# A turn of q moved ahead of the last half of w3, and the softmax sums of chunk 1 spread over the first down steps

## The chip, the cores and the metric

The kernel runs on one core of one Trainium2 chip. The core has a matrix engine (TensorE, PE in the profile), a vector engine (VectorE, DVE), a scalar engine for functions such as exp and ln (ScalarE, ACT), a general engine that here only issues loads and stores (GpSimd, POOL), a sync engine that issues transfers (SyncE, SP), and 16 DMA engines that move data between the chip's main memory and the on-chip memory. Matmuls write into PSUM, an accumulator memory of 8 banks, each 512 fp32 columns wide on 128 partitions; ScalarE and VectorE carry results from there to the on-chip memory. The metric is the time of one execution in microseconds, as the device measures it: a median of several runs, lower is better.

## The reference

Two stages follow each other: attention with projected keys and values, then a feed-forward layer that takes the maximum of three products.

```python
# q, k, v: (8 batches, 8 heads, 1024, 64) fp32;  E, F: (64, 1024)
k_proj = einsum('ks,bhsd->bhkd', E, k)             # 1024 keys become 64
v_proj = einsum('ks,bhsd->bhkd', F, v)
scores = matmul(q, k_proj.transpose(0, 1, 3, 2)) / 8
attn   = exp(scores - max);  attn = attn / (sum(attn) + 1e-9)
x      = matmul(attn, v_proj)                      # -> (8192 tokens, 512)
h      = maximum(maximum(x @ w1, x @ w2), x @ w3)  # w1, w2, w3: (512, 768)
out    = h @ w_out                                 # w_out: (768, 512)
```

## The kernel before: the parts that matter here

Each batch of 1024 tokens is worked off in two chunks of 512. From chunk 1 of batch 0 on there is a steady order: 18 steps of four matmuls (`l1`), four `down` steps, and between them, at fixed slots, the attention of the next batch. Chunk 0 of batch 0 has a path of its own, so that the matrix engine can start while the inputs still arrive. All loads that convert fp32 to bf16 go through one queue, in the order in which GpSimd issues them:

```python
for wt, w in zip(w_sb[1:], (w2, w3)):              # w2, w3 in halves of 256 rows
    for hh in range(2):
        nc.gpsimd.dma_start(out=wt[:, 2 * hh:2 * hh + 2, :], in_=w[hh * 256:(hh + 1) * 256]...)
# ... cut
nc.gpsimd.dma_start(out=q_1, in_=qv_[1])           # q of batch 0, chunk 1
for x in range(2):
    nc.gpsimd.dma_start(out=wo_sb[:, 3 * x:3 * x + 3], in_=...)   # w_out in halves
load(1, k, k_t); load(1, v, v_t); load(1, q, q_t)  # batch 1
```

The attention of chunk 1 of batch 0 has four parts. q is turned (d onto the partitions) by matmuls with the identity, into banks 4 to 7, and copied out:

```python
def q_up0():
    for g in range(NPAIR):                         # 4 pairs of heads: 32 matmuls in all
        for sl in range(4):
            for u in range(2):
                nc.tensor.matmul(out=ps[u * D:(u + 1) * D, 4 + g, sl * P:(sl + 1) * P],
                                 lhsT=q_1[:, HEAD[2 * g + u], sl, :], rhs=ident, ...)
    for j in range(2):                             # line 279: two banks in each copy
        nc.scalar.copy(out=qT[0][:, 4 + 2 * j:6 + 2 * j]..., in_=ps[:, 4 + 2 * j:6 + 2 * j, :]...)

def scores_up0():
    for g, bank in ((0, 4), (1, 5), (2, 6), (3, 7)):
        scores0(1, g, bank)                        # line 249, two matmuls each
    for g in (0, 2):                               # line 286, exp
        nc.scalar.activation(out=pT[:, g:g + 2, 1, :], in_=ps[:, 4 + g:6 + g, :], func=AF.Exp, scale=scale)

def sums0(ch, bank):
    quads0(ch, bank, lambda rows, g: ones[rows, :])                        # line 229
    nc.scalar.activation(out=lns[ch], in_=ps[:, bank:bank + 2, :], func=AF.Ln)          # line 257
    nc.scalar.activation(out=rinv[ch], in_=lns[ch], func=AF.Exp, scale=-1.0)            # line 258

def av_up0():
    for f, bank in enumerate((6, 4)):
        quads0(1, bank, lambda rows, g: vp2[0][rows, g, f, :])             # line 229
    norm0(1, 0, 6, (0, 1))                         # line 268, VectorE: xT = ps * rinv
    norm0(1, 1, 4, (0, 1))
```

The w2 and w3 steps of chunk 0 work in halves of the contraction, because the weights arrive in halves: first all steps with half 0, then with half 1, and a step that is complete goes to VectorE (line 405) and then ticks a slot.

```python
def l1_first(i, jts, banks):
    for hh in range(2):
        for jt, bank in zip(jts, banks):
            for ct in (2 * hh, 2 * hh + 1):
                nc.tensor.matmul(out=ps[:, bank, :], lhsT=w_sb[i][:, ct, ...], rhs=xT[0][:, ct, 0, :], ...)   # line 402
            if hh:
                nc.vector.tensor_tensor(out=h1c[jt] if i == 1 else hT[0][:, jt, :], ..., op=ALU.max)
                yield
```

Then comes `down` of chunk 0 in two halves of its contraction (`down_half`, line 216): four tiles of tokens with the first three tiles of h, then the same four with the last three. The slots at which the parts of attention go between:

```python
groups = [(10, q_up0), (11, scores_up0), (13, lambda: sums0(1, 4)), (15, av_up0),
          (19, g1[0]), (22, lambda: q_pe1(0)), (24, lambda: q_pe1(1)), (25, g1[1]), ...]   # g1: batch 1
...
for i, jts, banks in ((1, range(6), (6, 7, 0, 1, 4, 5)), (2, range(3), (2, 3, 6)), (2, range(3, 6), (0, 1, 2))):
    for _ in l1_first(i, jts, banks):
        tick()
state["f"] = 2
for x in range(2):
    for tt in range(4):
        down_half(tt, x)                           # bank (3 + tt) % 4
        if x:
            tick()
```

`g1[0]` is `kv` of batch 1 (lines 116 and 118): 16 matmuls into bank 4, which ScalarE and VectorE then empty in four copies (lines 122, 123, 125, 126). `q_pe1` turns half of the heads of batch 1's q with 16 transposes into banks 4 and 5 (line 299).

Of the kernel before, what the change touches and what calls it, by code (L numbers as in the profile page):

```python
# [16 lines left out]
def kernel(ctx: ExitStack, tc: tile.TileContext, q, k, v, E, F, w1, w2, w3, w_out, out):  # L17
    nc = tc.nc
# [13 lines left out]
    def T(shape, dt, name):  # L32
        return sb.tile(shape, dt, name=name)

    ps = pp.tile([P, 8, 512], FP32, name="ps")
# [7 lines left out]
    w_sb = [T([P, NCT, DF], BF16, f"w{i}_sb") for i in range(3)]  # L43
# [6 lines left out]
    qT = [T([P, H, SI // 2, P], BF16, f"qT{i}") for i in range(NB)]  # L50
# [20 lines left out]
    q_1 = q_t[0].rearrange("p h si d -> p (h si d)")[:, 4 * H * D:].rearrange("p (h n d) -> p h n d", h=H, d=D)  # L71
# [17 lines left out]
    def load_behind_turn(b, order="qkv"):  # L89

        nc.gpsimd.tensor_copy(out=seen, in_=kpT[(b - 1) % NB][:, 0, 0:1])
        for c in order:
            load(b, *{"q": (q, q_t), "k": (k, k_t), "v": (v, v_t)}[c])

    def q_turn(b, hs):
        nc.sync.dma_start_transpose(
            out=qT[b % NB][:, hs].rearrange("p h s t -> p (h s) t"),
            in_=q_t[b % NB][:, hs].rearrange("p h si d -> p (h si d)"),
        )
# [70 lines left out]
    state = {"f": 0, "n": 0}  # L170
# [40 lines left out]

    def down_half(tt, x):

        bank = (3 + tt) % 4
        for jt in range(3 * x, 3 * x + 3):
            nc.tensor.matmul(out=ps[:, bank, :], lhsT=hT[0][:, jt, tt * P:(tt + 1) * P],  # L216
                             rhs=wo_sb[:, jt, :], start=(jt == 0), stop=(jt == NJT - 1))
        if x:
            nc.scalar.copy(out=o_acc[0][:, tt, :], in_=ps[:, bank, :])
            if tt % 2 == 1:  # L220
                nc.gpsimd.dma_start(out=out_0[0][:, tt - 1:tt + 1, :], in_=o_acc[0][:, tt - 1:tt + 1, :])


    def quads0(ch, bank, lhs, hhs=(0, 1)):
        for hh, j, g, u in QUADS:
            if hh not in hhs:
                continue
            rows = slice(u * KP, (u + 1) * KP)
            nc.tensor.matmul(out=ps[j * HD:(j + 1) * HD, bank + hh, :], lhsT=lhs(rows, g),
                             rhs=pT[rows, g, ch, :], start=True, stop=True, tile_position=(u * KP, j * HD))  # L230
# [24 lines left out]
    def sums0(ch, bank):  # L255
        quads0(ch, bank, lambda rows, g: ones[rows, :])
        nc.scalar.activation(out=lns[ch], in_=ps[:, bank:bank + 2, :], func=AF.Ln)
        nc.scalar.activation(out=rinv[ch], in_=lns[ch], func=AF.Exp, scale=-1.0)  # L258
# [7 lines left out]
    def norm0(ch, half, bank, hhs):  # L266
        for hh in hhs:
            nc.vector.tensor_tensor(out=xT[0][:, 2 * hh + half, ch, :], in0=ps[:, bank + hh, :],  # L268
                                    in1=rinv[ch][:, hh * 512:(hh + 1) * 512], op=ALU.mult)


    def q_up0():
        for g in range(NPAIR):
            for sl in range(4):
                for u in range(2):
                    nc.tensor.matmul(out=ps[u * D:(u + 1) * D, 4 + g, sl * P:(sl + 1) * P], lhsT=q_1[:, HEAD[2 * g + u], sl, :],
                                     rhs=ident, start=True, stop=True)
        for j in range(2):
            nc.scalar.copy(out=qT[0][:, 4 + 2 * j:6 + 2 * j].rearrange("p h s t -> p (h s t)"),
                           in_=ps[:, 4 + 2 * j:6 + 2 * j, :].rearrange("p b n -> p (b n)"))  # L280

    def scores_up0():
        for g, bank in ((0, 4), (1, 5), (2, 6), (3, 7)):
# [4 lines left out]
    def av_up0():  # L288
        for f, bank in enumerate((6, 4)):
            quads0(1, bank, lambda rows, g: vp2[0][rows, g, f, :])  # L290
        norm0(1, 0, 6, (0, 1))
        norm0(1, 1, 4, (0, 1))


    def q_pe1(hh):
        for h in range(4 * hh, 4 * hh + 4):
            for sp in range(SI // 2):
                o = (h % 2) * 512 + sp * P
                nc.tensor.transpose(out=psb[:, AB + (h % 4) // 2, o:o + P],  # L299
                                    in_=q_t[1][:, h, 2 * sp:2 * sp + 2, :].rearrange("p s d -> p (s d)"), identity=ident)  # L300
        for j in range(2):
            (nc.vector.tensor_copy if j else nc.scalar.copy)(
                out=qT[1][:, 4 * hh + 2 * j:4 * hh + 2 * j + 2].rearrange("p h s t -> p (h s t)"), in_=psb[:, AB + j, :])
# [10 lines left out]
    qv_ = q[0].rearrange("h (ch p n) d -> ch p h n d", ch=2, p=P)  # L314
# [17 lines left out]
            load0(v, v_t, NPAIR - 1)  # L332
    for wt, w in zip(w_sb[1:], (w2, w3)):
        for hh in range(2):
            nc.gpsimd.dma_start(out=wt[:, 2 * hh:2 * hh + 2, :],
                                in_=w[hh * 256:(hh + 1) * 256].rearrange("(r f) n -> r f n", f=2))
    nc.vector.memset(ones, 1.0)  # L337
# [57 lines left out]
            nc.tensor.matmul(out=ps[:, W1B[jt], :], lhsT=w_sb[0][:, ct, jt * P:(jt + 1) * P], rhs=xT[0][:, ct, 0, :],  # L395
                             start=(ct == 0), stop=(ct == NCT - 1))

    def l1_first(i, jts, banks):
        for hh in range(2):
            for jt, bank in zip(jts, banks):  # L400
                for ct in (2 * hh, 2 * hh + 1):
                    nc.tensor.matmul(out=ps[:, bank, :], lhsT=w_sb[i][:, ct, jt * P:(jt + 1) * P], rhs=xT[0][:, ct, 0, :],  # L402
                                     start=(ct == 0), stop=(ct == NCT - 1))
                if hh:
                    nc.vector.tensor_tensor(out=h1c[jt] if i == 1 else hT[0][:, jt, :], in0=ps[:, bank, :], in1=h1c[jt],
                                            op=ALU.max)
                    yield
# [1 line left out]
    def av0(f, hh):  # L409
        quads0(0, 6 + f - hh, lambda rows, g: vp2[0][rows, g, f, :], (hh,))  # L410

    nc.gpsimd.dma_start(out=q_1, in_=qv_[1])
    for x in range(2):
        nc.gpsimd.dma_start(out=wo_sb[:, 3 * x:3 * x + 3], in_=w_out.rearrange("(jt p) m -> p jt m", p=P)[:, 3 * x:3 * x + 3])
    load(1, k, k_t)
# [28 lines left out]
    for b in range(B):  # L444
        groups = attention(b + 1, turn_dma) if b + 1 < B else []
        if b == 0:
            g1 = [g for _, g in groups]
            groups = [(10, q_up0), (11, scores_up0), (13, lambda: sums0(1, 4)), (15, av_up0),
                      (19, g1[0]), (22, lambda: q_pe1(0)), (24, lambda: q_pe1(1)), (25, g1[1]), (28, g1[2]),
                      (31, g1[3]), (32, g1[4]), (33, g1[5]), (34, g1[6]), (36, g1[7])]  # L450
        slot = 0
        gi = 0

        def tick():
            nonlocal slot, gi
            slot += 1
            while gi < len(groups) and groups[gi][0] <= slot:
                groups[gi][1]()
                gi += 1
            if b == 0:  # L460
                if slot == 22:
                    load_behind_turn(2, "kvq")
                if slot == 28:
                    q_turn(2, slice(0, H // 2))
                return
            if b == 1 and slot == 3:
                q_turn(2, slice(H // 2, H))
            if b + 2 < B:
                if slot == 9:
                    load_behind_turn(b + 2)  # L470
                if slot == 18:
                    q_turn(b + 2, slice(0, H // 2))
                if slot == 27:
                    q_turn(b + 2, slice(H // 2, H))

        for ch in range(2):
            c = 2 * b + ch
            if c == 0:
                for i, jts, banks in ((1, range(6), (6, 7, 0, 1, 4, 5)), (2, range(3), (2, 3, 6)), (2, range(3, 6), (0, 1, 2))):
                    for _ in l1_first(i, jts, banks):  # L480
                        tick()
                state["f"] = 2
                for x in range(2):
                    for tt in range(4):
                        down_half(tt, x)
                        if x:
                            tick()
                continue
            for s in range(18):
                l1(b, ch, c, s // 3, s % 3)  # L490
                tick()
                if pend and s in (2, 5, 8, 11):
                    pend.pop(0)()
                    tick()
            pend = [lambda tt=tt, b=b, ch=ch, c=c: down(b, ch, c, tt) for tt in range(4)]
        if b == 0:
            while pend:
                pend.pop(0)()
                tick()
# [32 lines left out]
```

The softmax here doesn't subtract the row's maximum and nothing guards it: scores larger than these inputs give would overflow.

## Time and profile before

| what | value |
|---|---|
| time, median of 3 runs | 401.62 us (401.57 to 401.82) |
| span of the profiled execution | 399.6 us |
| matrix engine busy | 392.9 us, 98% of the span |
| VectorE, ScalarE busy | 185.8 us, 166.5 us |
| granted clock of the matrix engine | 1.00 |
| the longest waits of matmuls | for VectorE's `ones` 1.2 us (1 time), for line 268 1.2 us (2 times) |

In a timeline, a row holds the start and the duration of a run of equal instructions in microseconds, the engine, the line of the kernel, the operation, the tiles that it writes and reads, and how many there are. In brackets stands how long the engine had been idle before, and what ended that. Matmuls are pipelined, so the durations of neighbouring rows overlap; the distance between two starts tells what a run costs. In the list of transfers, the last number is the time from issue to landing.

### The profile page before, as it was taken

The numbers are of one execution on the slowest core, as the hardware profiler recorded it, in microseconds if no ns is written. First come the engines' busy times: TensorE is split into PE (matmuls) and PEld (weight loads), VectorE is DVE, ScalarE is ACT, GpSimd is POOL, SyncE is SP. The second block draws the span as 40 slices with busy tenths as digits, with TensorE's granted clock in tenths as the row PEclk, the third lists the DMA queues.
The fourth block names the chain that finished last, engine by engine and source line by source line (L and its number), as shares of the span: only waits on it lengthen the run. The fifth ranks groups of instructions, "written<-read, shape, count | busy, mean of one in ns | idle before, by whom it ended". The sixth has DMA issues, their size and how long they took to land.

```text
span 399.6 us, 6013 instructions
## 1 busy us (share of the span) xinstructions
PE 392.9 (98%) x2432; PEld 170.0 (43%) x2432; DVE 185.8 (46%) x268; ACT 166.5 (42%) x250; POOL 71.6 (18%) x110
## 2 busy tenths in 40 slices
PE   8999899999999999999999999999999999999996
PEld 4444353444444444444444444444444444444443
DVE  3346355553744265433844256443655337433441
ACT  4413457347325552247223652245532472222222
POOL 7352140150002401060000600024010000000000
PEclk9999999999999999999999999999999999999999
DMA  8999969999922997259930899129991111102022
GB/s 219 206 209 205 206 170 204 228 146 179 181 91 66 168 179 181 64 97 192 226 121 13 166 196 219 53 65 175 216 137 62 59 52 54 52 2 105 1 107 105
DMA packets 62667, 53.73 MB, mean 134 GB/s; under 512 B 30512, under 2 KB 57648, under 8 KB 62640
## 3 DMA queue, kind: packets, MB, share of 16 engines
q0 software_dynamic: 31776, 43.52, 54.1%
q1 hardware_dynamic: 30032, 8.92, 15.8%
q10 hardware_dynamic: 832, 0.92, 0.7%
q8 instruction: 19, 0.31, 0.3%
q14 instruction: 8, 0.07, 0.0%
HBM read 57.15 MB, written 16.78 MB: 185 GB/s over the span
## 4 chain that ended last, share of the span: by engine, by line
PE 92%; DMA 4%; DVE 1%; ACT 1%; issue 1%; POOL 0%; POOLq 0%; DVEq 0%
PE ps L179 59%; PE ps L203 19%; PE ps L116 3%; PE ps L145 3%; PE ps L402 3%; DMA w_sb<-in_moe_w_dram 2%; DMA k_t<-in_k_dram 2%; PE ps L135 2%; PE ps L395 1%; PE ps L216 1%; DVE xT L160 1%; DVE xT L268 0%; PE ps L299 0%; PE ps L196 0%; ACT rinv L258 0%
## 5 line engine op out<-in xcount | busy, mean ns | idle before, releaser
L179 PE MATMUL ps<-xT,w_sb 128*128 128x512 bf16 x1080 | 246.6, 379 | 1.2 <-DVE xT L268 1.2
L179 PEld LDWEIGHTS <-w_sb 128*128 128x128 bf16 x1080 | 103.1, 98 | 133.9 <-issue 14.0
L184 DVE TENSOR_TENSOR m<-ps,h1s 128x512 f32<-128x512 f32 x90 | 62.2, 691 | 143.0 <-PE ps L179 114.8
L203 PE MATMUL ps<-wo_sb,hT 128*128 128x512 bf16 x354 | 85.5, 379 | 0.0
L182 ACT COPY h1s<-ps 128x512 f32<-128x512 f32 x90 | 52.8, 587 | 66.1 <-PE ps L179 65.8
L205 ACT COPY o_acc<-ps 128x512 f32<-128x512 f32 x59 | 34.6, 587 | 97.8 <-PE ps L203 97.8
L210 POOL DMA_DIRECT2D out_dram<-o_acc x28 | 20.1, 718 | 272.3 <-ACT o_acc L205 269.2
L186 DVE TENSOR_TENSOR hT<-ps,m 128x512 bf16<-128x512 f32 x90 | 62.3, 692 | 13.7 <-PE ps L179 5.2
L203 PEld LDWEIGHTS <-hT 128*128 128x128 bf16 x354 | 33.6, 98 | 44.1 <-issue 5.4
L160 DVE TENSOR_TENSOR xT<-ps,rinv 128x1024 bf16<-128x1024 f32 x28 | 32.9, 1217 | 7.8 <-PE ps L145 7.8
L138 ACT ACTIVATE pT<-ps 128x1024 bf16<-128x1024 f32 x28 | 27.1, 1021 | 13.3 <-PE ps L135 13.3
L87 POOL DMA_DIRECT2D v_t<-in_v_dram x21 | 15.3, 755 | 3.3 <-PE ps L402 2.5
L152 ACT ACTIVATE lns<-ps 128x1024 f32<-128x1024 f32 x14 | 13.6, 1021 | 1.9 <-PE ps L145 1.9
L155 ACT ACTIVATE rinv<-lns 128x1024 f32<-128x1024 f32 x14 | 14.2, 1061 | 0.0
L116 PE MATMUL ps<-k_t,eT 128*64 128x512 bf16 x56 | 13.4, 382 | 0.0
L118 PE MATMUL ps<-v_t,fT 128*64 128x512 bf16 x56 | 13.4, 382 | 0.0
L87 POOL DMA_DIRECT2D q_t<-in_q_dram x14 | 10.7, 770 | 3.9 <-DMA q_t<-in_q_dram 1.7
L87 POOL DMA_DIRECT2D k_t<-in_k_dram x14 | 10.6, 766 | 2.2 <-ACT o_acc L441 1.2
L402 PE MATMUL ps<-xT,w_sb 128*128 128x512 bf16 x48 | 10.9, 379 | 0.0
L122 ACT CAST kp<-ps 64x512 bf16<-64x512 f32 x7 | 4.1, 580 | 15.9 <-PE ps L118 15.9
L307 PE MATMUL ps<-warm 128*128 128x512 bf16 x26 | 9.4, 469 | 1.2 <-DVE ones L337 1.2
L123 DVE CAST kp<-ps 64x512 bf16<-64x512 f32 x7 | 4.8, 682 | 12.1 <-ACT kp L122 12.1
(84 smaller groups left out, 155.4 us busy)
## 6 DMA issues: line engine op xcount, KB each, us to landing
out_dram<-o_acc POOLq DMA_DIRECT2D x30, 512.0 KB, 3.3
q_t<-in_q_dram POOLq DMA_DIRECT2D x15, 512.0 KB, 8.8
k_t<-in_k_dram POOLq DMA_DIRECT2D x14, 512.0 KB, 13.3
v_t<-in_v_dram POOLq DMA_DIRECT2D x18, 256.0 KB, 17.5
v_t<-in_v_dram POOLq DMA_DIRECT2D x7, 512.0 KB, 16.8
w_sb<-in_moe_w_dram POOLq DMA_DIRECT2D x4, 384.0 KB, 10.2
k_t<-in_k_dram POOLq DMA_DIRECT2D x4, 256.0 KB, 8.1
w_sb<-in_moe_w_dram POOLq DMA_DIRECT2D x4, 192.0 KB, 9.8
```

Of the source, the lines that this page charges most:

```text
L87: nc.gpsimd.dma_start(out=dst[b % NB][:, slots], in_=sv[:, heads])
L116: nc.tensor.matmul(out=ps[0:KP, AB, :], lhsT=eT[:, si, :], rhs=k_t[i][:, :, si, :], start=(si == 0), stop=(si == SI - 1))
L138: nc.scalar.activation(out=pT[:, 2 * u + gg, :, :], in_=ps[:, AB + 2 * gg:AB + 2 * gg + 2, :], func=AF.Exp, scale=scale)
L160: nc.vector.tensor_tensor(out=xT[b % 3][:, 2 * u + half, :, :], in0=ps[:, AB + 2 * u:AB + 2 * u + 2, :], in1=rinv[u].rearrange("p (c n) -> ...
L179: nc.tensor.matmul(out=ps[:, bank, :], lhsT=w_sb[i][:, ct, jt * P:(jt + 1) * P], rhs=xT[b % 3][:, ct, ch, :], start=(ct == 0), stop=(ct == ...
L182: nc.scalar.copy(out=h1s[jt % 2], in_=ps[:, bank, :])
L184: nc.vector.tensor_tensor(out=m12[jt % 2], in0=ps[:, bank, :], in1=h1s[jt % 2], op=ALU.max)
L186: nc.vector.tensor_tensor(out=hT[c % 2][:, jt, :], in0=ps[:, bank, :], in1=m12[jt % 2], op=ALU.max)
L203: nc.tensor.matmul(out=ps[:, bank, :], lhsT=hT[c % 2][:, jt, tt * P:(tt + 1) * P], rhs=wo_sb[:, jt, :], start=(jt == 0), stop=(jt == NJT - 1))
L205: nc.scalar.copy(out=o[:, tt, :], in_=ps[:, bank, :])
L210: nc.gpsimd.dma_start(out=dst[:, tt - 1:tt + 1, :], in_=o[:, tt - 1:tt + 1, :])
L402: nc.tensor.matmul(out=ps[:, bank, :], lhsT=w_sb[i][:, ct, jt * P:(jt + 1) * P], rhs=xT[0][:, ct, 0, :], start=(ct == 0), stop=(ct == NCT ...
```

## The change

The change moves work in the first 50 us, with the same instructions in all but one place. The half of q for chunk 1 is loaded ahead of the last half of w3, so that it can be turned within the first w3 steps, after their first half of the contraction. The second of the two copies of turned q goes to VectorE. Scores follow the first three w3 steps, sums come after the last w3 step, and AV stands between the two halves of down. The aim is that exp, ln and normalisation of chunk 1 lie beside w3 and down matmuls. Banks are dealt anew so that banks 4 to 7 stay free for the attention meanwhile, and `kv` of batch 1 goes one slot later.

```diff
 def down_half(tt, x):
-        bank = (3 + tt) % 4
+        bank = tt
 ...  (q_up0)
         for j in range(2):
-            nc.scalar.copy(out=qT[0][:, 4 + 2 * j:6 + 2 * j]..., in_=ps[:, 4 + 2 * j:6 + 2 * j, :]...)
+            (nc.vector.tensor_copy if j else nc.scalar.copy)(
+                out=qT[0][:, 4 + 2 * j:6 + 2 * j]..., in_=ps[:, 4 + 2 * j:6 + 2 * j, :]...)
 ...  (loads)
     for wt, w in zip(w_sb[1:], (w2, w3)):
         for hh in range(2):
+            if wt is w_sb[2] and hh:
+                nc.gpsimd.dma_start(out=q_1, in_=qv_[1])
             nc.gpsimd.dma_start(out=wt[:, 2 * hh:2 * hh + 2, :], ...)
 ...
-    def l1_first(i, jts, banks):
+    def l1_first(i, jts, banks, between=None):
         for hh in range(2):
+            if hh and between:
+                between()
 ...
-    nc.gpsimd.dma_start(out=q_1, in_=qv_[1])
 ...  (slots)
-            groups = [(10, q_up0), (11, scores_up0), (13, lambda: sums0(1, 4)), (15, av_up0),
-                      (19, g1[0]), (22, lambda: q_pe1(0)), (24, lambda: q_pe1(1)), (25, g1[1]), ...
+            groups = [(9, scores_up0), (12, lambda: sums0(1, 4)), (20, g1[0]), (22, lambda: q_pe1(0)),
+                      (24, lambda: q_pe1(1)), (25, g1[1]), ...
 ...
-                for i, jts, banks in ((1, range(6), (6, 7, 0, 1, 4, 5)), (2, range(3), (2, 3, 6)), (2, range(3, 6), (0, 1, 2))):
-                    for _ in l1_first(i, jts, banks):
+                for part in ((1, range(6), (6, 7, 0, 1, 4, 5)), (2, range(3), (2, 3, 0), q_up0), (2, range(3, 6), (1, 2, 3))):
+                    for _ in l1_first(*part):
                         tick()
-                state["f"] = 2
+                state["f"] = 3
                 for x in range(2):
+                    if x:
+                        av_up0()
                     for tt in range(4):
                         down_half(tt, x)
```

More of the change, by code (lines that the diff above doesn't have):

```diff
@@ L278, in q_up0 @@
         for j in range(2):
-            nc.scalar.copy(out=qT[0][:, 4 + 2 * j:6 + 2 * j].rearrange("p h s t -> p (h s t)"),
-                           in_=ps[:, 4 + 2 * j:6 + 2 * j, :].rearrange("p b n -> p (b n)"))
+            (nc.vector.tensor_copy if j else nc.scalar.copy)(
+                out=qT[0][:, 4 + 2 * j:6 + 2 * j].rearrange("p h s t -> p (h s t)"),
+                in_=ps[:, 4 + 2 * j:6 + 2 * j, :].rearrange("p b n -> p (b n)"))
     def scores_up0():
@@ L447 @@
             g1 = [g for _, g in groups]
-            groups = [(10, q_up0), (11, scores_up0), (13, lambda: sums0(1, 4)), (15, av_up0),
-                      (19, g1[0]), (22, lambda: q_pe1(0)), (24, lambda: q_pe1(1)), (25, g1[1]), (28, g1[2]),
+            groups = [(9, scores_up0), (12, lambda: sums0(1, 4)), (20, g1[0]), (22, lambda: q_pe1(0)), (24, lambda: q_pe1(1)), (25, g1[1]), (28, g1[2]),
                       (31, g1[3]), (32, g1[4]), (33, g1[5]), (34, g1[6]), (36, g1[7])]
```

## The prediction

> **What bounds the kernel now.** I read the page first: the busy shares and the chain that ended last.
>
> ```profile
> PE 392.9 (98%) x2432; PEld 170.0 (43%) x2432; DVE 185.8 (46%) x268; ACT 166.5 (42%) x250; POOL 71.6 (18%) x110
> PE 92%; DMA 4%; DVE 1%; ACT 1%; issue 1%; POOL 0%; POOLq 0%; DVEq 0%
> ```
>
> TensorE is busy 98% of the span and carries 92% of the chain. So a change pays only through the time in which TensorE stands still, and all of that is near the start (a table by stretches gives 42.05 us busy of 42.10 from 57.9 to 100 us, then 100.00 of 100.00 twice). I therefore read TensorE's timeline of the stage that the diff touches: w2 and w3 steps, turn of q, scores, down, sums, AV, then chunk 1.
>
> ```profile
> 25.09 9.66 PE L402 MATMUL ps<-xT,w_sb 128*128 128x512 bf16 x44
> 34.69 1.08 PE L276 MATMUL ps<-ident,q_t 128*64 128x128 bf16 x32
> 35.70 0.60 PE L402 MATMUL ps<-xT,w_sb 128*128 128x512 bf16 x2
> 36.43 0.62 PE L249 MATMUL ps<-qT,kpT 64*64 64x512 bf16 x4
> 37.34 0.62 PE L249 MATMUL ps<-qT,kpT 64*64 64x512 bf16 x4 [0.29 <-ACT qT L279]
> 37.89 0.61 PE L402 MATMUL ps<-xT,w_sb 128*128 128x512 bf16 x2
> 38.34 3.40 PE L216 MATMUL ps<-wo_sb,hT 128*128 128x512 bf16 x15
> 41.67 0.41 PE L229 MATMUL ps<-pT,ones 64*32 64x512 bf16 x8
> 42.01 1.47 PE L216 MATMUL ps<-wo_sb,hT 128*128 128x512 bf16 x6
> 43.41 0.62 PE L229 MATMUL ps<-pT,vp 64*32 64x512 bf16 x16
> 43.97 0.82 PE L216 MATMUL ps<-wo_sb,hT 128*128 128x512 bf16 x3
> 45.15 0.38 PE L179 MATMUL ps<-xT,w_sb 128*128 128x512 bf16 x1 [0.36 <-DVE xT L268]
> 46.35 2.70 PE L179 MATMUL ps<-xT,w_sb 128*128 128x512 bf16 x11 [0.82 <-DVE xT L268]
> ```
>
> The durations overlap, so I count from start to start. The chain view gives 44 w2/w3 matmuls in 9.50 us, 0.216 us each. Dense cost from 25.26 us (where the chain puts the first w2 matmul) to the kv projection of batch 1 (49.05 us): 48 of w2/w3 10.36, turn 35.70-34.69 = 1.01, scores 2 x 0.55 (37.34 to 37.89) = 1.10, sums 0.34, AV 0.56, 24 down 5.18, 12 of chunk 1 2.59; together 21.14 us. The stretch takes 23.79, so 2.65 us are bubbles: 0.30 and 0.36 around the scores, 0.53 and 0.98 before the first two chunk 1 matmuls, and the rest small change at switches of operation. The two large ones end in the normalisation (DVE, line 268). Its own wait is in the next two views (ScalarE, then VectorE):
>
> ```profile
> 35.36 1.93 ACT L279 CAST qT<-ps 128x1024 bf16<-128x1024 f32 x2 [9.58 <-PE ps L276]
> 42.26 1.03 ACT L257 ACTIVATE lns<-ps 128x1024 f32<-128x1024 f32 x1
> 43.32 1.06 ACT L258 ACTIVATE rinv<-lns 128x1024 f32<-128x1024 f32 x1
> ...
> 44.41 2.48 DVE L268 TENSOR_TENSOR xT<-ps,rinv 128x512 bf16<-128x512 f32 x4 [5.18 <-ACT rinv L258]
> ```
>
> The sums ended at 42.01, so Ln, Exp and normalisation need until 46.89, while TensorE had only 9 down matmuls and AV to lay beside them.
>
> The change also swaps two loads, so I read issue-to-landing of single loads, in a short window each. The last half of w3 (384 KB, issued at 18.46 us), then the half of q (512 KB, 19.80 us):
>
> ```profile
> w_sb<-in_moe_w_dram POOLq DMA_DIRECT2D x1, 384.0 KB, 11.3
> ...
> q_t<-in_q_dram POOLq DMA_DIRECT2D x1, 512.0 KB, 12.7
> ```
>
> They landed at 29.76 and 32.50. The same reading gives 27.9 for w3's first half, 34.3 and 36.3 for w_out's halves, 46.5 for the last part of batch 1's v, 49.1 and 51.6 for its q: one unbroken stream, 1.9 us for 384 KB and 2.6 to 2.7 for 512 KB.
>
> **What the Trainium skill says.** "DMA: Bandwidth & Descriptors", section "Two DMAs through the same engine are not ordered": within one queue of one engine, descriptors start in order. The landings above are in the order of issue, so I let the two loads change places in the stream. "TensorE: Matmul & The Clock Gate", section "Back-to-back issue gap": about 216 ns for 512 columns on the warm clock; the trace has 0.216 us. "TensorEngine Tiling (Array Packing)", section "PSUM Bottleneck": use both ScalarE and VectorE to empty PSUM; that is what the split copy of turned q does, and before, ScalarE alone took 1.93 us for the pair. "PSUM — Partial Sum Buffer", section "Terms": two engines may not touch the same bank and quadrant at once. The trace agrees in so far as the readers of the kv bank go strictly one after another (below).
>
> **The change part by part.**
>
> Loads. The half of q goes in front of the last half of w3. It should land at 27.9 + 2.65 = 30.5 us, w3's half where q was, 32.4 to 32.5; w_out and all of batch 1 keep their times.
>
> Turn. It moves from behind 44 to behind 30 w2/w3 matmuls: 25.26 + 30 x 0.216 = 31.74 us. q is there since 30.5. Its second bank holds the last w2 step, which VectorE frees at 32.07 (its two L405 steps start at 30.79 and take 1.28), while TensorE wants it at 32.0: about 0.1 us lost. The turn ends near 32.85. The first w3 matmul of the second half needs w3 at 32.5: slack of 0.35 us.
>
> Copies. ScalarE takes 0.97 us (half of 1.93), about 32.6 to 33.6. VectorE's 128x1024 copy of fp32 has no row yet; a 1024-wide normalisation from PSUM takes 1217 ns on L160, and at 512 columns its copy (0.68) and its product (0.69) cost the same, so I estimate 1.2 us: 33.05 to 34.25. The six w3 matmuls between end at 34.15, and the third head pair, first to need the second copy, comes at 34.7. So the bubbles at the scores (0.66 us) go. The w3 maxima wait behind VectorE's copy, to about 36.2; the bank of the first is wanted again near 35.7 and is free by 35.0.
>
> Sums and AV. Scores end near 35.3, the last 12 w3 matmuls near 37.9, sums at 38.2. Both exponentials are done at about 36.9, so sums don't wait. Then 12 down matmuls (2.59 us) to 40.8; the Ln and Exp (2.1 us, from 38.35) end at 40.45 beside them. AV to 41.4, VectorE normalises from 41.2 to 43.7, and the second 12 down matmuls run to 44.0. So chunk 1's first matmul finds its columns: the two bubbles before it (1.51 us) go.
>
> Sum. The dense cost to kv with the 16 chunk 1 matmuls that now stand ahead of it is 22.0 us (21.14 + 4 x 0.216): 25.26 + 22.0 = 47.26, and I add 0.35 for the bank and the switches of operation: 47.6. Before, the same work would have been done at 49.05 + 0.86 = 49.9. Gain 2.3 us at this point.
>
> **What is given back.** After kv its bank is emptied by four copies in turn:
>
> ```profile
> 50.94 0.58 ACT L122 CAST kp<-ps 64x512 bf16<-64x512 f32 x1 [2.99 <-PE ps L118]
> 52.27 0.37 ACT L125 CAST vp<-ps 64x256 bf16<-64x256 f32 x1 [0.75 <-DVE kp L123]
> ...
> 51.55 0.68 DVE L123 CAST kp<-ps 64x512 bf16<-64x512 f32 x1 [1.76 <-ACT kp L122]
> 52.66 0.42 DVE L126 CAST vp<-ps 64x256 bf16<-64x256 f32 x1 [0.43 <-ACT vp L125]
> ```
>
> The bank is free at 53.08, 2.25 us behind kv's end (50.83). Then the turn of batch 1's q by TensorE writes it, and before, 12 matmuls (2.59 us) stood between. Now kv comes four matmuls later and the turn does not, so 8 are left, 1.73 us: TensorE waits about 0.5 us there. Net gain 2.3 - 0.5 = 1.8 us. Behind it the order is the same, TensorE has no bubble to lose, and loads and stores hang on the same slots: batch 2's last part of v landed at about 69 us for a kv at 76.3. So 1.8 us should reach the end: 401.6 - 1.8 = 399.8 us.
>
> **The rivals.**
> 1. The w3 load takes the place of the wait removed. For it: only 0.35 us of slack, and if w3 landed at 33.5 everything behind would move 0.65 us. Against: its place in the stream is fixed by bytes already measured. It would make 400.1 to 400.8.
> 2. Batch 1's loads become the bound. For it: kv moves from 49.05 to 47.6, and v lands at 46.5, a slack of 1.1 us; q lands at 49.1 for a turn at about 51.7. Against: both still fit. If the stream slipped by 2 us, kv would wait 0.9: 400.7.
> 3. The kv bank costs nothing, because VectorE's and ScalarE's copies come sooner than I think: gain 2.3, 399.3.
> 4. A copy on VectorE that takes much longer than 1.2 us delays scores and w3 maxima together: each 0.5 us over costs up to 0.5; I see nothing for it.
>
> **Range and chances.** The bubbles that the change can reach add up to 2.65 us, so 399.0 is a floor. Rivals 1 and 2 together cost about 1.5, which would leave a small gain; a loss needs more than one of them to be worse than worked out. I take 399.8 with 399.1 to 400.8. 2% is 8 us and no part of this stage holds so much: within 2% 0.985, faster 0.01, slower 0.005.
>
> **What would show it.** Right: no wait of chunk 1's first matmuls for line 268; the turn at 31.7 to 32 us, straight behind w2 and the first w3 half; Ln and Exp beside the first 12 down matmuls; kv's first matmul at about 47.6; a wait of 0.4 to 0.6 us before the first transpose of batch 1's q; the same distance from there to the end as before. Wrong: a TensorE wait for w_sb or q_t near 32.5 us, kv waiting for v_t, scores waiting for the VectorE copy by more than 0.3 us, or a new bubble behind 60 us.

## The result: 399.98 us, and the profile after

| | before | changed |
|---|---|---|
| time, median of 6 runs | 401.66 us (401.56 to 402.22) | 399.98 us (399.53 to 400.54) |
| changed / before | | 0.9958 (95% interval 0.9945 to 0.9971) |
| span of the profiled execution | 399.6 us | 398.1 us |

The changed kernel is 1.7 us, 0.4%, faster. Measured again beside other kernels it gave 0.9963 (0.9950 to 0.9976).

The page of the changed kernel, busy shares:

```profile
PE 392.5 (99%) x2432; PEld 170.0 (43%) x2432; DVE 186.9 (47%) x269; ACT 166.0 (42%) x249; POOL 71.6 (18%) x110
```

TensorE does the same work (392.5 us against 392.9) in a shorter span. Where the time came from is read in its timeline of the changed stage; lines 407, 276, 249, 229, 216 and 179 are w2 and w3 steps, turn, scores, sums or AV, down, and chunk 1; 116 and 300 are kv and the turn of batch 1's q. (An edit that adds or takes lines shifts these numbers by a few, so w3 steps are line 402 before and 405 or 408 in some experiments.)

```profile
25.15 6.64 PE L407 MATMUL ps<-xT,w_sb 128*128 128x512 bf16 x30
31.72 1.32 PE L276 MATMUL ps<-ident,q_t 128*64 128x128 bf16 x32
32.97 1.47 PE L407 MATMUL ps<-xT,w_sb 128*128 128x512 bf16 x6
34.37 1.05 PE L249 MATMUL ps<-qT,kpT 64*64 64x512 bf16 x8
35.35 2.76 PE L407 MATMUL ps<-xT,w_sb 128*128 128x512 bf16 x12
38.05 0.41 PE L229 MATMUL ps<-pT,ones 64*32 64x512 bf16 x8
38.39 2.76 PE L216 MATMUL ps<-wo_sb,hT 128*128 128x512 bf16 x12
41.08 0.62 PE L229 MATMUL ps<-pT,vp 64*32 64x512 bf16 x16
41.64 2.76 PE L216 MATMUL ps<-wo_sb,hT 128*128 128x512 bf16 x12
44.24 3.62 PE L179 MATMUL ps<-xT,w_sb 128*128 128x512 bf16 x16
47.79 0.40 PE L116 MATMUL ps<-k_t,eT 128*64 128x512 bf16 x1
...
49.64 1.90 PE L179 MATMUL ps<-xT,w_sb 128*128 128x512 bf16 x8
51.95 1.05 PE L300 MATMUL ps<-ident,q_t 128*128 128x128 bf16 x16 [0.42 <-DVE vp L126]
```

No row from 25 us on has a bracket until the last one: the two waits for the normalisation (0.36 and 0.82 us before) and the wait for the copy (0.29) are gone, and a new one stands before the turn of batch 1's q. ScalarE's and then VectorE's timeline show why the first chunk 1 matmul finds its columns:

```profile
38.53 1.02 ACT L257 ACTIVATE lns<-ps 128x1024 f32<-128x1024 f32 x1 [1.56 <-PE ps L229]
39.58 1.06 ACT L258 ACTIVATE rinv<-lns 128x1024 f32<-128x1024 f32 x1
...
33.07 1.22 DVE L279 CAST qT<-ps 128x1024 bf16<-128x1024 f32 x1 [0.95 <-PE ps L276]
41.62 2.49 DVE L268 TENSOR_TENSOR xT<-ps,rinv 128x512 bf16<-128x512 f32 x4 [2.45 <-PE ps L229]
```

Ln and Exp end at 40.6 us, beside the first 12 down matmuls, and VectorE waits for AV (2.45 us idle), no longer for Exp. It ends at 44.11, before chunk 1 begins at 44.24. The transfers, half of q issued at 18.52 us and last half of w3 at 19.85, each in a window of its own:

```profile
q_t<-in_q_dram POOLq DMA_DIRECT2D x1, 512.0 KB, 12.1
...
w_sb<-in_moe_w_dram POOLq DMA_DIRECT2D x1, 384.0 KB, 12.6
```

They land at 30.6 and 32.45 us: q 1.1 us ahead of its turn, w3 0.5 us ahead of its use (32.97).

The profiles begin this stage at slightly different times (25.09 us before, 25.15 after, 24.76 to 25.74 in the experiments other than w3_late); the last section comes back to this. So I compare the stretch from the first w2 matmul to the second turn of batch 1's q, behind which all orders are the same: 25.09 to 56.05 before, 30.96 us; 25.15 to 54.57 after, 29.42 us. From there to the end of the span it is about 343.5 us in both (the span is given to 0.1 us). The whole gain of the profiled execution is in that stretch: 1.54 us.

### The profile page after: what moved, and what is told of

It is laid out like the page before. It is cut to its first block, busy times and chain, and to the rows that moved or that the text cites. A ratio compares the mean times of both kernels' runs of the same rounds, so it can differ in the third digit from the quotient of the medians.

```text
span 398.1 us, 6013 instructions
## 1 busy us (share of the span) xinstructions
PE 392.5 (99%) x2432; PEld 170.0 (43%) x2432; DVE 186.9 (47%) x269; ACT 166.0 (42%) x249; POOL 71.6 (18%) x110
## 4 chain that ended last, share of the span: by engine, by line
PE 95%; DMA 2%; DVE 1%; ACT 0%; POOL 0%; issue 0%; POOLq 0%; DVEq 0%
PE ps L179 59%; PE ps L203 19%; PE ps L116 3%; PE ps L145 3%; PE ps L407 2%; DMA k_t<-in_k_dram 2%; PE ps L135 2%; PE ps L398 1%; PE ps L216 1%; PE ps L308 1%; PE ps L229 1%; DVE xT L160 1%; PE ps L249 1%; PE ps L300 0%; PE ps L242 0%; PE ps L196 0%
## 5 line engine op out<-in xcount | busy, mean ns | idle before, releaser
L152 ACT ACTIVATE lns<-ps 128x1024 f32<-128x1024 f32 x14 | 13.6, 1022 | 1.9 <-PE ps L145 1.9
```

## The experiments

All start from the changed kernel. "Stretch" is the one just described, from one profile of each kernel; the changed kernel has 29.42 us in both of its profiles. Ratios are to the kernel before on the same chip.

| run | time, us | ratio to before (95%) | stretch, us | against changed |
|---|---|---|---|---|
| sums_late | 401.83 | 1.0002 (0.9994 to 1.0011) | 31.09 | +1.67 |
| turn_late | 401.08 | 0.9990 (0.9981 to 0.9999) | 30.51 | +1.09 |
| loads_back | 400.54 | 0.9973 (0.9962 to 0.9983) | 30.01 | +0.59 |
| kv19 | 399.36 | 0.9945 (0.9930 to 0.9960) | 28.84 | -0.58 |
| copy_act | 400.11 | 0.9957 (0.9940 to 0.9973) | 29.42 | 0.00 |
| w3_late | 427.13 | 1.0627 (1.0606 to 1.0647) | not comparable | |
| turn_order | 399.47 | 0.9941 (0.9926 to 0.9957) | 29.18 | -0.24 |
| kv19_order | 399.46 | 0.9940 (0.9922 to 0.9959) | 28.80 | -0.62 |
| w3_behind_wo | 401.49 | 0.9996 (0.9986 to 1.0005) | 30.89 | +1.47 |
| kv18 | 400.05 | 0.9959 (0.9944 to 0.9974) | 29.93 | +0.51 |
| four_first | 399.56 | 0.9947 (0.9929 to 0.9964) | 28.61 | -0.81 |
| after_again | 400.39 | 0.9963 (0.9950 to 0.9976) | 29.42 | 0.00 |

**sums_late: sums and AV back to their old slots**

```diff
-groups = [(9, scores_up0), (12, lambda: sums0(1, 4)), (20, g1[0]), ...
+groups = [(9, scores_up0), (13, lambda: sums0(1, 4)), (15, av_up0), (20, g1[0]), ...
 for x in range(2):
-    if x:
-        av_up0()
```

> Only the place of sums and AV of chunk 1 is undone: sums after the first tile of the second down half, AV after its third, as before; the early turn stays. My theory (the two bubbles before chunk 1 come from Ln, Exp and normalisation having too little matmul work beside them): the bubbles of 0.4 and 0.8 us before chunk 1's first two matmuls return, kv of batch 1 starts near 49.3 us instead of 47.8, the time is about 1.5 us over the changed kernel, 401.4 us. Rival (the early turn made the gain, the placement of sums and AV matters little): 400.0 to 400.3 us.

TensorE's timeline of this run, the first chunk 1 matmuls:

```profile
45.33 0.38 PE L179 MATMUL ps<-xT,w_sb 128*128 128x512 bf16 x1 [0.36 <-DVE xT L268]
46.53 3.56 PE L179 MATMUL ps<-xT,w_sb 128*128 128x512 bf16 x15 [0.82 <-DVE xT L268]
```

The two waits return with exactly the sizes that they had before the change, and the time is that of before. The rival, that the early turn alone made the gain, falls: here the turn is early and nothing is left of the gain. The early turn does give something, 0.44 us: from the first w2 matmul to chunk 1's first matmul it is 19.62 us here (25.71 to 45.33) and 20.06 before. It is more than paid again at the new wait before the turn of batch 1's q, which this kernel has too (0.42 us by its bracket, 0.59 from start to start). Whether the early turn alone would have kept its 0.44 us with kv at its old slot was not tried.

**turn_late: load order and place of the turn undone, sums and AV stay**

```diff
-groups = [(9, scores_up0), (12, lambda: sums0(1, 4)), ...
+groups = [(10, q_up0), (11, scores_up0), (12, lambda: sums0(1, 4)), ...
-(2, range(3), (2, 3, 0), q_up0)
+(2, range(3), (2, 3, 0))
 # and the load of q_1 behind w3, as before
```

> Sums and AV stay where the change puts them; the load order and the place of the turn are undone (turn after four of the six w3 steps, scores a step later). My theory (the early turn is needed so that exp is over before the sums): scores wait for the copies, sums wait about 1 us for exp, chunk 1 starts without a wait for the normalisation; kv about 1.2 to 1.6 us later than in the changed kernel, 401.3 us. Rival (AV between the halves is the whole gain, the turn may stay late): 400.0 to 400.3 us.

TensorE's timeline; the row is the sums:

```profile
39.23 0.41 PE L229 MATMUL ps<-pT,ones 64*32 64x512 bf16 x7 [0.51 <-ACT pT L287]
```

Chunk 1 starts without a wait, but the sums wait for exp, and the stretch is 1.09 us longer, a little less than I expected. AV between the halves is not the whole gain: with the sums straight behind the last w3 step, it needs the scores early, and so the early turn. Whether a late turn with the sums some matmuls later would do as well was not tried. The two losses, 1.67 and 1.09 us, add up to more than the gain of 1.54, as each was measured with all the rest in place.

**loads_back: only the order of the two loads undone**

```diff
-            if wt is w_sb[2] and hh:
-                nc.gpsimd.dma_start(out=q_1, in_=qv_[1])
 ...
+    nc.gpsimd.dma_start(out=q_1, in_=qv_[1])       # ahead of w_out
```

> Only the order of the two loads is undone; the turn stays within the w3 steps. My theory: q lands near 32.5 us, the turn would start at 31.7, so TensorE waits 0.8 us there, in place of the 0.3 us for the bank; about 0.5 us over the changed kernel, 400.5 us. Rival (the order of the loads is hidden by slack): 400.0 us, no wait for q_t.

TensorE's timeline, the turn:

```profile
32.55 1.08 PE L276 MATMUL ps<-ident,q_t 128*64 128x128 bf16 x32 [0.76 <-DMA q_t<-in_q_dram]
```

As expected: the turn starts 0.82 us later behind the first w2 matmul than in the changed kernel (a wait of 0.76 us for q by the bracket), of which the bank's wait gives 0.23 back (the row costs 1.02 us from start to start, and 1.25 in the changed kernel). The order of the loads is worth 0.6 us.

**kv19 and kv18: kv of batch 1 one and two slots earlier**

```diff
-(20, g1[0])
+(19, g1[0])        # kv18: (18, g1[0])
```

> Only kv of batch 1 goes back one slot, so that 12 matmuls stand before it and 12 behind it. My theory (TensorE waits 0.42 us for the emptying of kv's bank before it turns batch 1's q): that wait is gone, kv starts at 46.9 us, half a microsecond behind the landing of v at 46.4; 0.4 us under the changed kernel, 399.6 us. Rival (the later slot is needed because v of batch 1 has not landed): TensorE waits for v_t before kv by 0.3 to 0.6 us, and the time stays at 400.0 us.

> kv of batch 1 goes two slots earlier than in the changed kernel, with 8 matmuls before it and 16 behind it. My theory (with kv one slot earlier the wait for kv's bank is gone and v of batch 1 still lands in time, but two slots earlier it does not): kv would start at 45.9 us, TensorE waits 0.5 to 0.7 us for v_t (46.4 us): about 400.0 us, 0.6 over the kernel with kv one slot earlier. Rival (v has more slack): no wait for v_t, 399.4 us.

kv19, TensorE's timeline from the 12 matmuls behind kv to the turn:

```profile
48.54 2.76 PE L179 MATMUL ps<-xT,w_sb 128*128 128x512 bf16 x12
51.14 1.06 PE L300 MATMUL ps<-ident,q_t 128*128 128x128 bf16 x16
```

No bracket: the wait for kv's bank is gone, and the stretch is 0.58 us shorter, more than the 0.42 in the bracket. From start to start, 8 matmuls and the wait had taken 2.31 us (49.64 to 51.95) where the 8 alone take 1.73. kv starts at 46.69 and v's last part lands at 46.55 (issued at 31.15, 15.4 us), so it just fits. kv18, the same view:

```profile
45.67 0.40 PE L116 MATMUL ps<-k_t,eT 128*64 128x512 bf16 x1
46.79 0.38 PE L118 MATMUL ps<-v_t,fT 128*64 128x512 bf16 x1 [0.71 <-issue]
```

The first matmul, which needs k, runs, and the second, which needs v, stands until 46.79. The bracket names "issue", as the profile found no releaser, but v's last part landed at 30.84 + 15.9 = 46.74 us. So kv one slot earlier is free, and two slots earlier costs 1.09 us of stretch against that, more than the bracket and more than the 0.6 that I expected: the second matmul starts 1.12 us behind the first, and this profile began the stage 0.16 us sooner than kv19's while v landed 0.19 us later. The load of v is the next bound.

**copy_act: both copies of turned q on ScalarE**

```diff
-(nc.vector.tensor_copy if j else nc.scalar.copy)(out=qT[0]...)
+nc.scalar.copy(out=qT[0]...)
```

> Only the split of the two copies of turned q is undone: both on ScalarE. My theory: they run from 32.6 to 34.6 us, the scores of the third head pair come at 34.8, so the split buys almost nothing: 400.0 to 400.1 us, and the w3 maxima come 1.2 us sooner on VectorE. Rival (the split is needed to take the bubble at the scores away): scores wait 0.3 to 0.5 us for qT, 400.4 us.

ScalarE's two copies take from 32.38 to 34.31 us (x2, 1.93 us), and TensorE's rows have no wait; the stretch is the same to the hundredth. With six w3 matmuls between turn and scores, the split of the copies is worth nothing. The advice of the Trainium skill ("TensorEngine Tiling (Array Packing)", section "PSUM Bottleneck") to empty PSUM with both engines bought nothing here, as no matmul waited for the copies.

**turn_order: the heads in banks 6 and 7 turned first**

```diff
-for g in range(NPAIR):
+for g in (2, 3, 0, 1):
```

> Only the order in which the turn works off the pairs of heads is changed: those in banks 6 and 7 first, those in banks 4 and 5, which the last two w2 steps leave last, behind them. My theory (the changed kernel loses 0.3 us in the turn, because its second bank is not yet free): the turn takes 1.0 us instead of 1.3, 0.3 us under the changed kernel, 399.7 us. Rival (that time only moves to the next wait, as the first bank's copy now comes last and the scores begin with it): scores wait 0.2 to 0.3 us for qT, 400.0 us.

TensorE's timeline, turn and the row behind it:

```profile
31.47 1.08 PE L276 MATMUL ps<-ident,q_t 128*64 128x128 bf16 x32
32.48 1.47 PE L407 MATMUL ps<-xT,w_sb 128*128 128x512 bf16 x6
```

1.01 us from start to start against 1.25 in the changed kernel. Nothing takes the 0.24 us back.

**kv19_order and four_first: the edits together**

kv19_order is both edits above. four_first adds a split of the six w3 steps into four and two:

```diff
-(2, range(3), (2, 3, 0), q_up0), (2, range(3, 6), (1, 2, 3))
+(2, range(4), (2, 3, 0, 1), q_up0), (2, range(4, 6), (2, 3))
```

> Both: kv one slot earlier and banks 6 and 7 first in the turn. My theory: 0.3 us plus 0.4 us under the changed kernel, 399.3 us, unless kv, which would start at 46.6 us, meets the landing of v at 46.4 to 46.5 us. Rival (v of batch 1 bounds it): TensorE waits for v_t and the gains don't add, 399.6 us.

> kv one slot earlier, banks 6 and 7 first in the turn, and four instead of three w3 steps in the first group, so that two more matmuls stand ahead of the need for w3's last half. My theory (with both earlier edits TensorE met the landing of w3, a wait of 0.18 us): that wait is gone and the two gains add up to 0.8 us under the changed kernel: 399.2 us, unless kv meets the landing of v at 46.4 us. Rival (the next load in the stream bounds it): waits for v_t take the place, 399.4 us.

In kv19_order the stretch is 0.62 us shorter, 0.20 less than the two edits give apart (0.58 and 0.24), but not for the reason that I gave (v). TensorE's timeline, and the piece directly ahead of its second row in the chain of waits:

```profile
31.46 1.08 PE L276 MATMUL ps<-ident,q_t 128*64 128x128 bf16 x32
32.65 1.47 PE L407 MATMUL ps<-xT,w_sb 128*128 128x512 bf16 x6
...
19.60 13.01 DMA w_sb<-in_moe_w_dram
```

The turn ends at 32.47, w3 lands at 32.61, and the next row starts at 32.65. This is not an effect of the two edits together: up to chunk 1 this kernel does the same as turn_order, whose stage began at the same time (24.90 us against 24.89). There the load of w3, issued at 19.30 us, took

```profile
w_sb<-in_moe_w_dram POOLq DMA_DIRECT2D x1, 384.0 KB, 12.8
```

and landed at 32.1 us, ahead of its use at 32.48. So the landing moved by half a microsecond between two executions, which is as much as its slack. In four_first, two more matmuls stand ahead of w3's use, the turn goes over into the next row in 1.02 us, and the stretch is 0.81 us shorter, the sum of both edits. That the split did this is not shown: this profile began the stage late (25.74 us, with a wait of 1.1 us for the first k), and w3 landed at 32.7 us, 1.1 us ahead of its use at 33.76, so two matmuls less would not have met it either. In time, the four kernels with these edits can't be told apart: their intervals overlap, and their medians are 399.36 to 399.56. All four beat the kernel before clearly, and have medians under the changed kernel; which of them is best is open.

**w3_late and w3_behind_wo: a load put ahead of the last half of w3**

```diff
 nc.gpsimd.dma_start(out=q_1, in_=qv_[1])
+nc.gpsimd.dma_start(out=k_t[1][:, 0:4], ...)        # w3_late; taken out further down
+nc.gpsimd.dma_start(out=wo_sb[:, 0:3], ...)         # w3_behind_wo; taken out further down
```

> The first half of batch 1's k (512 KB, needed anyway) is moved ahead of the last half of w3 as well; the sum of bytes is the same. My theory (one queue works in order, w3 lands about 0.5 us ahead of its use in the changed kernel): w3 lands near 35.1 us, TensorE waits 2.1 us for it, and nothing takes that up later: 402.1 us. Rival (the load's place has more slack than I read, or later waits shrink with it): TensorE waits less than 1.5 us, or the time stays under 401.3 us.

> The first half of w_out (384 KB, needed from 38.4 us on) is moved ahead of the last half of w3; the sum of bytes is the same and no memory is shared. My theory (one queue works in order, w3 lands about 0.5 us ahead of its use in the changed kernel): w3 lands near 34.3 us, TensorE waits 1.3 to 1.4 us for it, nothing takes that up later: 401.3 us. Rival (the load has more slack than I read, or later waits shrink with it): a wait of under 0.9 us, or a time under 400.8 us.

w3_late says nothing on its question, by my own mistake: the memory of batch 1's k also holds chunk 0's q in fp32 at the start, and the early load stands ahead of the casts of that q in the program. So the casts read memory into which k had been loaded (this kernel computes with other data), and waited for that load: the first turn of q on TensorE waits 25.8 us. w3_behind_wo asks the same with a load that shares nothing. TensorE's timeline:

```profile
34.48 1.47 PE L408 MATMUL ps<-xT,w_sb 128*128 128x512 bf16 x6 [1.41 <-DMA w_sb<-in_moe_w_dram]
```

384 KB ahead moved w3 from 32.45 to 34.43 us (issued at 20.83, 13.6 us), TensorE waited 1.41, the stretch grew by 1.47, and the gain of the change was all but gone. So a load put ahead in this queue moves the next by its share of the stream, 1.98 us where I had read 1.9 for 384 KB, and nothing behind makes up for a late w3.

## Why the prediction was right, point by point

- **The bubbles.** Right. The stage had 2.65 us of them by the chain (2.75 by the timeline, 23.89 less 21.14), the two before chunk 1 came from Ln, Exp and normalisation, and both they and those at the scores are gone. sums_late shows that the first two hang on the place of sums and AV.
- **Loads.** Right: 30.6 and 32.45 us where I had 30.5 and 32.4 to 32.5. The first rival had a slack of 0.35 us, measured 0.5; w3_behind_wo shows that it was a real danger. The slack is not fixed: it was 0.9 us in the second profile of the changed kernel, 0.2 in kv19, and used up in kv19_order.
- **Turn and copies.** The start (31.72, where I had 31.74) was right, by some luck: the first w2 matmul starts at 25.15 us in the timeline and not at the chain's 25.26, and the 30 matmuls take 6.57 us and not 6.48. The term for the bank was too small, 0.1 us, measured 0.24 (turn_order). VectorE's copy took 1.22 us where I had estimated 1.2, so the fourth rival did not come up; copy_act shows that the split itself mattered for nothing.
- **Gain up to kv.** The term mis-sized is the 0.35 us added for bank and switches. From the first w2 matmul to kv it is 22.64 us (25.15 to 47.79) against a dense 22.0, so 0.64: 0.24 for the bank, and 0.4 in all for switches of operation. Five runs of full-width matmuls take about 0.1 us each over their dense cost (the 12 before the sums 2.70 us, those before AV 2.69, where 12 x 0.216 is 2.59), and the scores give 0.1 back (0.98 from start to start, where I had 1.10). The gain at that point is 2.11 us, not 2.3: before, it is 23.89 us by the timeline (25.09 to 48.98), and four matmuls more make 24.75. The dense rate itself held, 44 matmuls in 9.50 us. The section of the Trainium skill that I named for it ("TensorE: Matmul & The Clock Gate", section "Back-to-back issue gap") gives about 216 ns for a matmul on its own and about 131 ns in a stream of weight loads and matmuls. The trace has such a stream, with as many weight loads as matmuls, at 216 ns, so the 131 does not hold here.
- **Given back.** Right in kind: the wait stands before the turn of batch 1's q and is released by the last of the four copies. I had 0.5, it is 0.58 (2.31 us from start to start for 8 matmuls that take 1.73), which also refutes the third rival.
- **To the end.** Right: 343.5 us behind the stretch in both. The second rival, batch 1's loads as bound, was not reached, but kv18 finds it one slot beyond kv19.
- **Sum.** 1.8 us predicted, 1.68 by the medians, 1.54 by the stretches of single profiles. Both terms were a little too good (2.3 for 2.11, 0.5 for 0.58); the interval of the times, 1.2 to 2.2 us of gain, can't tell 1.5 from 1.8.

## What to carry to other kernels

When the matrix engine is busy 98% of the time, look for its bubbles by start-to-start distances, and ask for each which chain on the other engines ends it. A chain such as Ln, Exp and normalisation (4.6 us here) is hidden by placing its start that much matmul work ahead of its use, and that in turn may hang on a load order. Count what a shift takes away elsewhere: moving kv by four matmuls left too little work to cover the emptying of its bank, and gave back 0.58 of the 2.11 us that the change had won up to there.

## What the runs showed of the hardware that was not expected

Going from full-width matmuls (128x128 weights, 512 columns) to an operation with smaller weights costs TensorE about 0.1 us that no bracket shows. In the changed kernel, 12 such matmuls take 2.70 us from start to start ahead of the sums and 2.69 ahead of AV (64x32 weights), but 2.60 where the next operation is full-width too (down to chunk 1, 41.64 to 44.24). In kv19 they take 2.68 ahead of kv (128x64 weights), and 2.60 ahead of the turn of batch 1's q, whose weights are 128x128 again. What the 0.1 us consists of was not tried.

And the time of one kernel moves by some tenths of a microsecond before this stage begins: the changed kernel's first k matmuls waited for k by 0.39 and 0.23 us in one profile and 0.76 and 0.34 in the other, and its w2 steps began at 25.15 and 25.59 us. The landing of k is not the only cause. sums_late, which began at 25.71 us, has no wait for k; there eight transposes and four matmuls behind them took 2.64 us (7.61 to 10.25), where copy_act took 1.44 (7.46 to 8.90). Why is open.
